# Loading q, k and v in rows of 1 KB, with part of the opening loads moved to ScalarE

## The chip, the cores and the metric

The kernel runs on one core of a Trainium2 chip. The metric is the device time of one execution in microseconds; the median of three runs before the change is 470.75 us (470.01 to 472.14). Engines are called by their short names: PE (TensorE matmuls), PEld (its weight loads), ACT (ScalarE), DVE (VectorE), POOL (GpSimd) and SP (SyncE, which here only issues DMAs; SPq is its sequencer). The engines run their own instruction lists in order and wait for one another through semaphores.

## What is computed

Two layers stand one behind the other. The first is a retention layer without softmax: for 8 batches and 8 heads of 64, over 576 positions, the causal scores are weighted by a power of a per-head decay.

```
scores = scale * q @ k.T
ret    = scores * (gamma ** (i - j) where i >= j else 0)
attn   = ret @ v
```

The second takes that result as `x` (8 x 576 x 512) into a mixture of 4 attention experts, of which each position uses the best 2.

```
w = softmax of the 2 largest of x @ w_gate
for e in range(4):
    q, k, v = x @ wq[e], x @ wk[e], x @ wv[e]
    a = causal softmax(scale * q @ k.T)
    out += w[e] * (a @ v @ wo[e])
```

## The kernel before, in words

The 576 positions of a batch are 9 chunks of 64, and two chunks make a tile. There are 36 tiles (`NT`) of 128 positions, and three tiles make a group, of which there are 12 (`NG`). For each tile n the kernel loads two blocks of 512 KB: `x` (q and k transposed, `load(n, 0)`, tensor `xf`) and `vk` (v and k, `load(n, 1)`, tensor `vkf`). In both, each of 128 partitions receives one run of 4 KB. The pool holds 3 `x` buffers and 4 `vk` buffers, so tile n+3 can only be loaded into `x` when tile n has been read.

The first layer is worked chunk by chunk. `qk(n)` (L130) multiplies q and k of a chunk on PE; ACT copies the result out (`p<-qk`, L144) and POOL zeroes what lies above the diagonal (L147). `decay(n)` (L101) multiplies v by decay factors, on DVE for the first tiles and on POOL later. `state(n)` (L109, `st`) adds a chunk's k-v product to a running sum, kept by DVE (L128). `old(n)` (L152) multiplies q by the sum of all earlier chunks, and ACT copies that out (`x<-old`, L169). `own(n)` (L171) multiplies the chunk's own scores by v, and DVE adds it (L188). `scale(n)` (L200) multiplies by a table `gi`. `split(n)` (L202) rounds the result to a shorter float on ACT (`xh`, L210) and keeps the rest on POOL (`xl`, L211), so that the second layer's projections run as three matmuls each on `xh` and `xl`.

The second layer is a pipeline by group. At stage j, group j-1 is projected (`proj`, `pj`, L250; `vproj`, `pv`, L274), group j-2 goes through scores, softmax and values, and group j-3 through the output projection (`po`, L473), whose tiles SP stores (L477). The opening, called the head here, is j = 0: three tiles of the first layer with no second-layer work on PE. The first `pj` block follows tiles 0 to 2 and needs their `xh` and `xl`, and the weights `k` and `q`, split into `wh` and `wl` by `weights` (ACT L235, then DVE or POOL L236).

Eight PSUM banks go round, mostly two to a step. The first two `pj` outputs take over the two banks of `qk(4)`, so they need ACT's copy `p<-qk` of tile 4.

PE, DVE, ACT and POOL run in the order in which the code writes the work. SP's order is the scheduler's. All loads, of tiles, weights (`fetch`), tables (`gi`, `con`, `mask`) and the gate's weights (`rg`) are issued by SP. Up to eight DMAs are tracked at a time, each by one of eight semaphores: a ninth waits for the first to have landed.

Of the kernel before, what the change touches and what calls it, by code (L numbers as in the profile page):

```python
# [22 lines left out]
NT = 9 * NP  # L23
# [4 lines left out]
def f(ap):  # L28
    return ap.bitcast(F32)
# [9 lines left out]
def units(g):  # L39
    out = []  # L40
    for n in range(3 * g, 3 * g + 3):
        out += [(n, 0), (n, 1)] if n % 9 == 8 else [(n, None)]
    return out
# [3 lines left out]
def kernel(ctx: ExitStack, tc: tile.TileContext, xf, vkf, wraw, gi_d, con_d, out):  # L47
    nc = tc.nc
# [8 lines left out]
    v = nc.vector  # L57
# [25 lines left out]
    HALF = [slice(0, 64), slice(64, 128)]  # L83
    X, VK, P, S_, XR = {}, {}, {}, {}, {}

    def load(n, w):
        if n >= NT:
            return
        if w == 0:
            X[n] = x = ld.tile([128, 2, 4, 128], F32, name="x", tag="x")  # L90
            nc.sync.dma_start(x, xf[n])
        else:
            VK[n] = vk = ld.tile([128, 2, 2, 4, D], F32, name="vk", tag="vk", bufs=4)
            nc.sync.dma_start(vk, vkf[n])

    def table(c):
        t0, C = 128 * c, 128 if c < 4 else 64
# [3 lines left out]
    def decay(n, e=None):  # L101
        if n >= NT:
            return
        vv = VK[n][:, :, 0]
        k = chunks(n)[0][1]
        gm = gam[:, 8:9] if k == 8 else gam[:, k:k + 2]
        (e or gp).tensor_mul(vv, vv, gm.unsqueeze(3).to_broadcast([128, 2, 4, D]))  # L107
# [22 lines left out]
    def qk(n):  # L130
        if n >= NT:
            return
        x = X[n]
        ps = [bank([128, 2, 2, 64], "qk") for g in range(2)]
        for s in range(2):
            i = slice(64 * s, 64 * s + 64)
            for u in range(2):
                for g in range(2):
                    for r in range(2):
                        h = 2 * r + u  # L140
                        mm(ps[g][HALF[r], s, u], x[HALF[g], 1, h, i], x[HALF[g], 0, h, i], start=True, stop=True)  # L141
        P[n] = p = sa.tile([128, 2, 2, 2, 64], F32, name="p", tag="p")
        for g in range(2):
            act(p[:, g], ps[g], AF.Copy)  # L144
        for r in range(2):
            w = p[HALF[r]].rearrange("p g s u i -> p (g s u) i")
            gp.affine_select(w, w, pattern=[[0, 8], [1, 64]], base=0, channel_multiplier=-1,  # L147
                             compare_op=OP.is_ge, fill=0.0)
# [3 lines left out]
    def old(n):  # L152
        if n >= NT:
            return
        ps = [bank([128, 2, 128], "old") for g in range(2)]
        x = X[n]
        R[n] = x32 = sa.tile([128, 2, 2, 128], F32, name="x32", tag="x32", bufs=2)
        ch = chunks(n)
        f0 = 64 if ch[0][1] == 0 else 0
        for s, (b, k) in enumerate(ch):  # L160
            i = slice(64 * s, 64 * s + 64)
            if k:
                for r in range(2):
                    for g in range(2):
                        for u in range(2):
                            mm(ps[g][HALF[u], r, i], S_[b, k - 1][HALF[g], r, u], x[HALF[g], 0, 2 * r + u, i],  # L166
                               start=True, stop=True)
        for g in range(2):
            act(x32[:, g, :, f0:], ps[g][:, :, f0:], AF.Copy)  # L169
# [32 lines left out]
    def split(n, e=None):  # L202
        if n >= NT:
            return
        g, l0 = n // 3, 128 * (n % 3)
        if n % 3 == 0:
            XR[g] = (sa.tile([128, 4, GW], F32R, name="xh", tag="xh"), sa.tile([128, 4, GW], F32R, name="xl", tag="xl"))
        xh, xl = XR[g]
        x32 = R.pop(n).rearrange("p g r i -> p (g r) i")
        act(xh[:, :, l0:l0 + 128], x32, AF.Copy)  # L210
        (e or gp).tensor_sub(xl[:, :, l0:l0 + 128], x32, f(xh[:, :, l0:l0 + 128]))  # L211
# [6 lines left out]
    TSZ = {1: 11 * 128, 2: 15 * 128, 3: 9 * 128, 4: 9 * 128}  # L218
    rg = const.tile([128, 4, E], F32, name="rg")

    def fetch(w):
        o, kc, n = WCUT[w]
        z = {"k": 1, "q": 2, "v": 3, "o": 4}[w]
        RAW[w] = raw = sb.tile([128, PSZ[z]], F32, name="raw", tag=f"p32{z}")[:, :kc * n].rearrange("p (k w) -> p k w", k=kc)
        nc.sync.dma_start(raw, wraw[:, o:o + kc * n].rearrange("p (k w) -> p k w", k=kc))

    def weights(w, e=None):
        o, kc, n = WCUT[w]
        raw = RAW[w]
        wt = n if w != "v" else NWV  # L230
        hi = const.tile([128, kc, wt], F32R, name="wh" + w)
        lo = const.tile([128, kc, wt], F32R, name="wl" + w)
        W[w] = (hi, lo)
        for r, cs in [(raw, slice(0, n))] + ([(rg, slice(n, wt))] if w == "v" else []):
            act(hi[:, :, cs], r, AF.Copy)  # L235
            (e or v).tensor_sub(lo[:, :, cs], r, f(hi[:, :, cs]))  # L236
# [243 lines left out]
    def run(*gs):  # L480
        for g in gs:
            for _ in g:
                pass

    def stage(j, i):
        g, o = j - 1, j - 3
        if 0 <= g < NG:
            if i == (0 if j == 1 else 2):
                for p in range(2):
                    for w in "kq":  # L490
                        yield from proj(g, w, p)
            else:
                for ti in (2,) if i == 1 else (0, 1):
                    yield from vproj(3 * g + ti)
        if 0 <= o < NG and i < 2:
            for d in (2 * i, 2 * i + 1):
                yield from outproj(o, d)
# [8 lines left out]
    load(2, 0)  # L506
    load(2, 1)
    fetch("k")
    fetch("q")
    nc.sync.dma_start(rg, wraw[:, 4096:].rearrange("p (k w) -> p k w", k=4))  # L510
    load(3, 1)
    fetch("v")
    nc.sync.dma_start(mask[:, 512:], con_d[:, 220:])
    decay(0, v)
    qk(0)
    state(0)
    for j in range(NG + 3):
        us = units(j - 2) if 0 <= j - 2 < NG else []
        for i in range(3):
            n = 3 * j + i  # L520
            if n < 2:
                decay(n + 1, v)
            if n != 2:
                qk(n + 1)
            old(n)
            work = stage(j, i)
            here = us[i:i + 1] if i < 2 else us[2:]
            soft = [scores(u) for u in here[:1]]
            for sc in soft:
                next(sc)  # L530
            own(n)
            if n == 2:
                qk(3)
            state(n + 1)
            for u in here[1:]:
                soft.append(scores(u))
                next(soft[-1])
            load(n + 3, 0)
            load(n + 4, 1)
            if n == 0:  # L540
                fetch("o")
            scale(n, v if n < 3 else None)
            if 2 < n + 2 and i < 2:
                decay(n + 2)
            for u, sc in zip(here, soft):
                for _ in sc:
                    next(work, None)
                normal(u)
            split(n)
            if 0 < n + 1 < 5:  # L550
                table(n + 1)
            if i == 2:
                decay(n + 2)
            if n == 1:
                weights("k")
            if n == 2:
                weights("q", gp)
                weights("v")
            if n == 5:
                weights("o")  # L560
            run(work)
        for u in us:
            run(turn(u))
        if 0 <= j - 1 < NG:
            gate(j - 1)
        for u in us:
            values(u, u[0] == NT - 1)


def _layout(inputs):  # L570
    q, k, v = (np.asarray(inputs[n]) for n in "qkv")
    qk = np.stack([q, k], 1).reshape(B, 2, 2, 4, S, D)
    qkt = qk.transpose(0, 2, 5, 1, 3, 4).reshape(B, 128, 2, 4, 9, 64)
    vk = np.stack([v, k], 1).reshape(B, 2, 2, 2, 2, 9, 64, D).transpose(0, 5, 3, 6, 1, 2, 4, 7).reshape(B, 9, 128, 2, 4, D)
    xf = np.stack([np.stack([qkt[b, :, :, :, c] for b, c in chunks(n)], 3) for n in range(NT)]).reshape(NT, 128, 2, 4, 128)
    vkf = np.stack([np.stack([vk[b, c] for b, c in chunks(n)], 1) for n in range(NT)])
    wq, wk, wv = (np.asarray(inputs["moe_w" + n]).transpose(1, 0, 2).reshape(DM, E * D) for n in "qkv")
    wg = np.asarray(inputs["moe_w_gate"])
    wo = np.asarray(inputs["moe_wo"]).reshape(2, 128, DM).transpose(1, 0, 2).reshape(128, 2 * DM)
    cut = [w.reshape(4, 128, -1).transpose(1, 0, 2).reshape(128, -1) for w in (wq, wk, wv, wg)]  # L580
    wraw = np.ascontiguousarray(np.concatenate(cut[:3] + [wo, cut[3]], 1))
    return {"xf": np.ascontiguousarray(xf), "vkf": np.ascontiguousarray(vkf), "wraw": wraw}


def _tables():
# [38 lines left out]
```

## Time and profile before

| what | value |
|---|---|
| median of 3 runs | 470.75 us |
| profiled execution, its own time | 470.5 us |
| its span (first to last instruction) | 468.5 us |
| busy share of the span: PE, PEld, ACT, DVE, POOL | 93%, 85%, 61%, 58%, 46% |
| HBM read | 40.26 MB |
| DMA, mean over the span | 109 GB/s |
| granted clock, mean over the span | 0.967 |

So 2.0 us of the profiled execution lie outside its span. A busy share is a mean over stages with different limits. What the head is worth is read from its own windows, from the chain of waits (which follows the last work back to what released it) and from the timeline, whose rows give the start, the duration, the engine, the line, the operation and, in brackets, the idle time before it with what ended that. "issue" in a chain or a bracket is time in which the engine waited for nothing that the profile shows. Starts are microseconds from the span's beginning.

### The profile page before, as it was taken

What the parts mean: (1) busy time and instruction counts of PE and PEld (TensorE: products, weight loads), DVE (VectorE), ACT (ScalarE), POOL (GpSimd) and SP (SyncE); (2) the same over time, 40 slices, a digit from 0 to 9 for tenths busy, and PEclk for the clock granted to TensorE, in tenths of its full rate; (3) what the DMA queues carried; (4) which work ended last, traced back from release to release, by engine and by line L of the source; (5) the groups of instructions that cost most, each with busy time, mean ns of one, the idle gap of its engine ahead of it and who ended that gap; (6) DMA issues with size and microseconds to landing.
All of it is one profiled execution on the core that took longest, in us unless ns stands there. A gap on an engine that the chain in (4) does not pass through costs nothing.

```text
span 468.5 us, 18762 instructions
## 1 busy us (share of the span) xinstructions
PE 436.8 (93%) x7876; PEld 397.9 (85%) x7876; DVE 273.0 (58%) x1069; ACT 286.4 (61%) x834; POOL 216.1 (46%) x272
## 2 busy tenths in 40 slices
PE   7589879999999999999999999999999999999786
PEld 4478769889879989889979999889979999897476
DVE  1562773864685654864775654854775654746650
ACT  2545466584685476584686576685686576664752
POOL 5477665563653555563653455553553453202001
PEclk8769899999999999999999999999999999999869
DMA  8953441242252153252352153242241010010101
GB/s 286 406 200 105 171 135 48 93 160 91 92 186 65 50 186 110 92 165 86 94 167 83 41 193 111 92 163 88 93 162 44 5 52 18 2 69 2 69 0 69
DMA packets 18899, 50.89 MB, mean 109 GB/s; under 512 B 2304, under 2 KB 9088, under 8 KB 18816
## 3 DMA queue, kind: packets, MB, share of 16 engines
q1 hardware_dynamic: 18816, 49.71, 31.3%
q8 instruction: 62, 1.02, 0.9%
q14 instruction: 21, 0.17, 0.1%
HBM read 40.26 MB, written 9.44 MB: 106 GB/s over the span
## 4 chain that ended last, share of the span: by engine, by line
PE 79%; ACT 7%; DVE 4%; DMA 4%; issue 3%; POOL 1%; SPq 1%; ACTq 0%; POOLq 0%; DVEq 0%
PE pj L250 22%; PE pv L274 11%; PE pt L419 8%; PE po L473 8%; PE ss L348 7%; PE ys L445 6%; PE own L183 4%; DMA x<-xf 4%; PE qk L141 4%; PE st L119 3%; PE old L166 2%; ACT p L379 2%; PE ys L452 2%; DVE sm L391 2%; PE ys L449 2%
## 5 line engine op out<-in xcount | busy, mean ns | idle before, releaser
L211 POOL TENSOR_TENSOR xl<-x,xh 128x512 fp32r<-128x512 f32 x36 | 46.1, 1280 | 89.3 <-ACT xh L210 89.3
L379 ACT ACTIVATE p<-p,nm 128x128 f32<-128x128 f32 (+8 forms) x144 | 79.7, 559 | 10.4 <-DVE nm L368 9.5
L368 DVE CUSTOM_DVE_ANT_0 p<-ss,mask 128x128 f32<-128x128 f32 (+7 forms) x128 | 51.0, 454 | 29.0 <-PE ss L348 28.5
L463 POOL CAST yh<-y 128x256 fp32r<-128x256 f32 (+1 forms) x38 | 14.4, 380 | 106.4 <-ACT y L462 106.4
L399 ACT ACTIVATE p<-p,sm 128x64 f32<-128x64 f32 (+4 forms) x72 | 37.0, 556 | 42.0 <-DVE sm L393 42.0
L423 DVE COPY pth<-pt 128x512 f32<-128x512 f32 (+2 forms) x52 | 31.4, 618 | 48.2 <-PE pt L419 47.8
L147 POOL TENSOR_SCALAR_AFFINE_SELECT p<-p 64x512 f32<-64x512 f32 x72 | 48.7, 676 | 20.3 <-ACT p L144 17.7
L419 PE MATMUL pt<-con,p 128*128 128x128 f32 x360 | 45.1, 287 | 5.4 <-DVE nm L373 3.3
L419 PEld LDWEIGHTS pt<-con,p 128*128 128x128 f32 x360 | 43.3, 149 | 6.1 <-DVE nm L373 3.4
L200 POOL TENSOR_TENSOR x<-x,gi 128x512 f32<-128x512 f32 x29 | 37.4, 1290 | 20.4 <-DVE x L188 19.5
L348 PE MATMUL ss<-k,q 64*64 64x64 f32 (+7 forms) x512 | 41.7, 409 | 2.2 <-ACT ot L476 2.2
L183 PEld LDWEIGHTS own<-p,vk 64*64 64x64 f32 x1152 | 28.5, 142 | 13.4 <-issue 10.4
L445 PE MATMUL ys<-pth,vn 128*64 128x128 f32 (+1 forms) x640 | 39.8, 257 | 0.0
L183 PE MATMUL own<-p,vk 64*64 64x64 f32 x1152 | 30.4, 229 | 6.6 <-ACT xh L210 2.8
L107 POOL TENSOR_TENSOR vk<-vk,con 128x512 f32<-128x512 f32 x33 | 35.4, 1074 | 0.3 <-DMA vk<-vkf 0.3
L391 DVE TENSOR_SCALAR sm<-sm 128x4 f32<-128x4 f32 (+1 forms) x40 | 15.5, 388 | 30.6 <-ACT p L379 30.0
L425 ACT ACTIVATE pth<-pt 128x512 f32<-128x512 f32 (+2 forms) x52 | 27.2, 541 | 9.3 <-PE pt L419 9.3
L210 ACT ACTIVATE xh<-x 128x512 fp32r<-128x512 f32 x36 | 22.2, 617 | 17.2 <-POOL x L200 9.6
L445 PEld LDWEIGHTS ys<-pth,vn 128*64 128x64 f32 x640 | 29.6, 139 | 1.5 <-issue 1.5
L401 DVE TENSOR_SCALAR p<-p,sm 128x64 f32<-128x64 f32 (+4 forms) x104 | 29.1, 333 | 1.4
L141 PEld LDWEIGHTS qk<-x 64*64 64x64 f32 x1152 | 21.6, 141 | 9.6 <-issue 7.0
L119 PE MATMUL st<-vk 64*64 64x64 f32 x1024 | 25.8, 232 | 4.3 <-DVE vk L107 2.2
(94 smaller groups left out, 1069.8 us busy)
## 6 DMA issues: line engine op xcount, KB each, us to landing
x<-xf SPq DMA_DIRECT2D x36, 512.0 KB, 4.0
vk<-vkf SPq DMA_DIRECT2D x36, 512.0 KB, 5.3
out<-ot SPq DMA_DIRECT2D x48, 192.0 KB, 2.0
raw<-wraw SPq DMA_DIRECT2D x4, 512.0 KB, 9.4
gi<-gi SPq DMA_DIRECT2D x1, 256.0 KB, 8.1
con<-con SPq DMA_DIRECT2D x1, 110.0 KB, 3.9
mask<-con SPq DMA_DIRECT2D x1, 32.0 KB, 8.5
rg<-wraw SPq DMA_DIRECT2D x1, 8.0 KB, 9.3
```

What stands on the lines that cost most here:

```text
L119: mm(ps[r][HALF[g], s, u], vk[HALF[r], s, 1, h], vk[HALF[r], s, 0, h], start=True, stop=True)
L141: mm(ps[g][HALF[r], s, u], x[HALF[g], 1, h, i], x[HALF[g], 0, h, i], start=True, stop=True)
L147: gp.affine_select(w, w, pattern=[[0, 8], [1, 64]], base=0, channel_multiplier=-1, compare_op=OP.is_ge, fill=0.0)
L183: mm(ps[r][HALF[u], g, i], vk[HALF[r], s, 0, 2 * g + u], p[HALF[r], g, s, u], start=True, stop=True)
L211: (e or gp).tensor_sub(xl[:, :, l0:l0 + 128], x32, f(xh[:, :, l0:l0 + 128]))
L250: mm(ps, ww[:, kc, p * 128:(p + 1) * 128], xx[:, kc, c], start=(i == 0), stop=(i == 11))
L274: mm(ps, xx[:, kc, l0:l0 + 128], ww[:, kc], start=(i == 0), stop=(i == 11))
L348: mm(ps[e][HALF[p]], q[p][HALF[z], l0 + 64 * s:l0 + 64 * s + 64], k[p][HALF[z], kb:kb + ws[e]], start=True, stop=True)
L368: v.tensor_tensor_reduce(p32[:, e, :ws[e]], ps[e], mask[:, 576 - ws[e]:], -1.0, BIG, OP.add, OP.min, nm[:, e:e + 1])
L379: act(p32[:, e, :ws[e]], p32[:, e, :ws[e]], AF.Exp, bias=bias[e], scale=-1.0, accum_out=sm[:, 0, e:e + 1])
L419: nc.tensor.transpose(pt[:, i], src, ident)
L445: mm(py[HALF[z], p], VN[n0 + j][:, e * D:(e + 1) * D], src, start=(j == 0), stop=False)
```

## The change

Three things are done.

1. The host lays `xf` and `vkf` out so that a tile's block is four pieces of 128 rows of 1 KB, and the loads read them so. A partition still receives 4 KB, as four runs of 1 KB. All 72 loads are changed, over the whole run.
2. At the opening SP issues fewer loads: the blocks of tiles 0 to 3 and the weights `k` and `q`. `x` of tile 3 is now issued in the opening, ahead of the loop.
3. The blocks of tile 4, `rg` and the weight `v` are issued by ACT behind `split(1)`; the blocks of tile 5, `vk` of tile 6 and the weight `o` by ACT behind `split(2)`. From tile 3 on, SP issues the loads at the same places as before. The weight `v` is split into `wh` and `wl` one tile later.

```diff
-    def load(n, w):
+    def load(n, w, e=None):
+        e = e or nc.sync
...
-            nc.sync.dma_start(x, xf[n])
+            e.dma_start(x.rearrange("p a h i -> p (a h i)").rearrange("p (c w) -> p c w", c=4), xf[n].rearrange("c p w -> p c w"))
...
-            nc.sync.dma_start(vk, vkf[n])
+            e.dma_start(vk.rearrange("p s a h d -> p (s a h d)").rearrange("p (c w) -> p c w", c=4), vkf[n].rearrange("c p w -> p c w"))
...
     fetch("k")
     fetch("q")
-    nc.sync.dma_start(rg, wraw[:, 4096:].rearrange("p (k w) -> p k w", k=4))
+    load(3, 0)
     load(3, 1)
-    fetch("v")
     nc.sync.dma_start(mask[:, 512:], con_d[:, 220:])
...
-            load(n + 3, 0)
-            load(n + 4, 1)
-            if n == 0:
-                fetch("o")
+            if n > 2:
+                load(n + 3, 0)
+                load(n + 4, 1)
...
             split(n)
+            if n == 1:
+                load(4, 0, nc.scalar)
+                load(4, 1, nc.scalar)
+                nc.scalar.dma_start(rg, wraw[:, 4096:].rearrange("p (k w) -> p k w", k=4))
+                fetch("v", nc.scalar)
+            if n == 2:
+                load(5, 0, nc.scalar)
+                load(5, 1, nc.scalar)
+                load(6, 1, nc.scalar)
+                fetch("o", nc.scalar)
...
             if n == 2:
                 weights("q", gp)
+            if n == 3:
                 weights("v")
...
+    xf, vkf = (np.ascontiguousarray(a.reshape(NT, 128, 4, 256).transpose(0, 2, 1, 3)) for a in (xf, vkf))
```

The orders below are of one engine each, at three places. Line numbers of the change are one higher than before for the same step.

SP in the opening, before, from `x` of tile 2 to `x` of tile 3 (`raw` is a weight, in the order k and q, v, o):

```order
L91 DMA x<-xf 128x1024
L94 DMA vk<-vkf 128x1024
L225 DMA raw<-wraw 128x1024 x2
L510 DMA rg<-wraw 128x16
L94 DMA vk<-vkf 128x1024
L225 DMA raw<-wraw 128x1024
L513 DMA mask<-con 128x64
L225 DMA raw<-wraw 128x1024
L91 DMA x<-xf 128x1024
```

The same stretch with the change; of the last row's two, the first is `x` of tile 3 and the second `x` of tile 6:

```order
L92 DMA x<-xf 128x4x256
L95 DMA vk<-vkf 128x4x256
L226 DMA raw<-wraw 128x1024 x2
L95 DMA vk<-vkf 128x4x256
L513 DMA mask<-con 128x64
L92 DMA x<-xf 128x4x256 x2
```

Two weights and `rg` no longer stand ahead of `x` of tile 3. All that stands ahead of `x` of tile 2 is as it was.

ACT from `xh` of tile 1 to the copies of tile 2, before:

```order
L210 ACTIVATE xh<-x_312 128x4x128
L99 ACTIVATE gi<-gi,con 128x128 x4
L235 ACTIVATE whk<-raw 128x1024
L169 ACTIVATE x_393<-old 128x256 x2
L144 ACTIVATE p<-qk 128x256 x2
```

and with the change:

```order
L211 ACTIVATE xh<-x_305 128x4x128
L92 DMA x<-xf 128x4x256
L95 DMA vk<-vkf 128x4x256
L552 DMA rg<-wraw 128x16
L226 DMA raw<-wraw 128x1024
L100 ACTIVATE gi<-gi,con 128x128 x4
L236 ACTIVATE whk<-raw 128x1024
```

Four DMA issues now stand on ACT between `xh` of tile 1 and the table, and so ahead of the split of the weight `k`.

ACT from `xh` of tile 2 to the copy of `qk(4)`, before:

```order
L210 ACTIVATE xh<-x_393 128x4x128
L99 ACTIVATE gi<-gi,con 128x128 x4
L235 ACTIVATE whq<-raw 128x1024
L235 ACTIVATE whv<-raw 128x4x256
L235 ACTIVATE whv<-rg 128x4x4
L144 ACTIVATE p<-qk 128x256 x2
```

and with the change:

```order
L211 ACTIVATE xh<-x_389 128x4x128
L92 DMA x<-xf 128x4x256
L95 DMA vk<-vkf 128x4x256 x2
L226 DMA raw<-wraw 128x1024
L100 ACTIVATE gi<-gi,con 128x128 x4
L236 ACTIVATE whq<-raw 128x1024
L145 ACTIVATE p<-qk 128x256 x2
```

Four DMA issues have come in ahead of the copy of `qk(4)`, and the two copies of `whv` have left. On PE and POOL the order is the same as before; on DVE the two steps of `wlv` stand behind the additions of tile 3 instead of ahead of them.

More of the change, by code (lines that the diff above doesn't have):

```diff
@@ L219, with fetch @@
     rg = const.tile([128, 4, E], F32, name="rg")
-    def fetch(w):
+    def fetch(w, e=None):
         o, kc, n = WCUT[w]
@@ L224, in fetch @@
         RAW[w] = raw = sb.tile([128, PSZ[z]], F32, name="raw", tag=f"p32{z}")[:, :kc * n].rearrange("p (k w) -> p k w", k=kc)
-        nc.sync.dma_start(raw, wraw[:, o:o + kc * n].rearrange("p (k w) -> p k w", k=kc))
+        (e or nc.sync).dma_start(raw, wraw[:, o:o + kc * n].rearrange("p (k w) -> p k w", k=kc))
     def weights(w, e=None):
@@ L581, in _layout @@
     wraw = np.ascontiguousarray(np.concatenate(cut[:3] + [wo, cut[3]], 1))
-    return {"xf": np.ascontiguousarray(xf), "vkf": np.ascontiguousarray(vkf), "wraw": wraw}
+    xf, vkf = (np.ascontiguousarray(a.reshape(NT, 128, 4, 256).transpose(0, 2, 1, 3)) for a in (xf, vkf))
+    return {"xf": xf, "vkf": vkf, "wraw": wraw}
 def _tables():
```

## The prediction

> **What bounds the kernel now.** I read first the busy time by stretches, since a share over the whole span hides the head.
>
> ```profile
> core 0: us, PE busy (x) PEld busy (x) DVE busy (x) ACT busy (x) POOL busy (x), PEclk, DMA share, GB/s
> ...
> 12.00:32.00 20.00, 12.51 (x410) 11.46 (x399) 10.33 (x26) 11.68 (x31) 10.98 (x11) 0.66 0.82 315
> 32.00:72.00 40.00, 34.16 (x761) 31.09 (x760) 24.40 (x94) 20.60 (x71) 27.19 (x27) 0.95 0.42 138
> 72.00:390.00 318.00, 312.96 (x5846) 289.42 (x5846) 197.42 (x793) 207.23 (x611) 160.81 (x194) 1.00 0.32 104
> ```
>
> From 72 us on PE is busy for 312.96 of 318 us while DMA is at 0.32. There PE is the bound, a load that takes longer has cover, and whatever the head gains or loses is carried to the end. Only the head has room: from 12 to 32 us PE works 12.51 of 20 us at a granted clock of 0.66, with DMA at 0.82. So I read the chain of waits there.
>
> ```profile
> 3.83 8.66 DMA x<-xf
> 13.32 1.76 issue
> 16.87 8.78 DMA x<-xf
> 25.79 1.12 PE qk L141 x28
> 26.90 1.51 issue
> 31.46 9.00 PE pj L250 x48
> ```
>
> Two loads carry it: x of tile 2, issued at 3.83 and landed at 12.49, and x of tile 4, issued at 16.87 and landed at 25.65. PE starts qk of tile 4 0.14 us after. The first projection, pj, starts at 31.4 us. But a chain shows one limit where there may be two, so I follow ACT, and below it DVE, to the same point.
>
> ```profile
> 20.01 0.63 ACT L210 ACTIVATE xh<-x 128x512 fp32r<-128x512 f32 x1 [2.91 <-DVE x L200]
> 20.55 1.26 ACT L99 ACTIVATE gi<-gi,con 128x128 f32<-128x128 f32 x4
> 21.71 1.04 ACT L235 ACTIVATE whk<-raw 128x1024 fp32r<-128x1024 f32 x1
> ...
> 27.11 0.63 ACT L210 ACTIVATE xh<-x 128x512 fp32r<-128x512 f32 x1 [2.07 <-DVE x L200]
> 27.65 1.26 ACT L99 ACTIVATE gi<-gi,con 128x128 f32<-128x128 f32 x4
> 28.82 1.04 ACT L235 ACTIVATE whq<-raw 128x1024 fp32r<-128x1024 f32 x1
> 29.76 1.04 ACT L235 ACTIVATE whv<-raw 128x1024 fp32r<-128x1024 f32 x1
> ...
> 30.81 0.63 ACT L144 ACTIVATE p<-qk 128x256 f32<-128x256 f32 x2
> ```
>
> ```profile
> 22.79 1.22 DVE L236 TENSOR_TENSOR wlk<-raw,whk 128x1024 fp32r<-128x1024 f32 x1 [2.87 <-ACT whk L235]
> 23.93 0.74 DVE L188 TENSOR_TENSOR x<-x,own 128x256 f32<-128x256 f32 x2
> 25.23 0.88 DVE L128 TENSOR_TENSOR s<-st,s 128x128 f32<-128x128 f32 x4 [0.56 <-PE st L119]
> 26.04 0.98 DVE L200 TENSOR_TENSOR x<-x,gi 128x512 f32<-128x512 f32 x1
> ```
>
> This is a second chain with almost no slack. It goes from xh of tile 1 over whk to DVE's wlk, the additions of own (L188) and st (L128) and scale (L200), and back to ACT's xh of tile 2 and p<-qk of tile 4. Each row starts when the one before ends, but for 0.56 us that DVE waits for st. The first pj needs the bank that p<-qk of tile 4 empties, and starts 0.6 us after that copy. The change puts eight DMA issues on exactly this chain.
>
> **The change part by part.** All sums are made against the profiled execution: 468.5 us of span in 470.5 us, 0.25 us under the median of the runs.
>
> *Rows of 1 KB, transfer.* The trace has no such row, so I take the rows on both sides of it, in three short windows: 4 KB alone, 512-byte rows of gi, 1.5 KB rows of the output.
>
> ```profile
> q1 hardware_dynamic: 561, 2.04, 102.7%
> ...
> DMA packets 390, 0.29 MB, mean 366 GB/s; under 512 B 14, under 2 KB 362, under 8 KB 390
> ...
> q1 hardware_dynamic: 390, 0.29, 109.6%
> ...
> q1 hardware_dynamic: 576, 0.79, 34.9%
> ```
>
> The columns of a queue's row are packets, MB and the share of 16 DMA engines' time. The first window is 5 us: 1.027 x 16 x 5 = 82.2 us of DMA time for 2.04 MB, which is 498 rows of 4 KB (the other packets are tiny and I leave them out): 165 ns each, 1.32 us for a load's 8 rows on each engine. The second is 0.8 us: 14.0 us, less 28 rows of 4 KB at 165, leaves 9.4 us for 348 rows of 512 B, 27 ns. The third is 6 us: 33.5 us for 0.79 MB, 514 rows of 1.5 KB, 65 ns. On the line between, 1 KB is 46 ns, four of them 184 ns, 12% over 165. A load's 32 rows on an engine then take 1.47 us where the queue is full, 0.15 us more. Five loads stand up to and with x of tile 2 (x0, vk0, x1, vk1, x2), none is taken away ahead of it: it lands 0.75 us later, and the chain through it starts 0.75 us later. Bounds: nothing, or 1.1 us if 1 KB costs two rows of 512 B, as gi's.
> A page of the Trainium skill, DMA: Bandwidth & Descriptors (section Why small descriptors are slow), gives a fixed cost of about 3 cycles per packet beside one per 32 bytes. By it four rows of 1 KB take 140 cycles against 131, 7%, and the shift would be an estimated 0.45 us; the rows of gi cost more than that, so I keep the rows.
>
> *Two weights and rg off the opening.* x of tile 3 has two weights less in front (2 x 1.32 us) and eight loads of 1 KB rows (8 x 0.15), so it lands 1.4 us earlier. What that frees:
>
> ```profile
> 21.61 1.05 PE L183 MATMUL own<-p,vk 64*64 64x64 f32 x32 [2.77 <-ACT xh L210]
> 23.23 1.13 PE L141 MATMUL qk<-x 64*64 64x64 f32 x32 [0.56 <-DMA x<-xf]
> 24.11 1.10 PE L119 MATMUL st<-vk 64*64 64x64 f32 x32
> ```
>
> The 0.56 us before qk of tile 3 goes. With the 0.75 above, own starts at 22.36, qk at 23.42, st at 24.30 and ends at 25.4.
>
> *Tile 4 from ACT.* The load is issued with xh of tile 1, at 20.01 + 0.75 = 20.8, when the queue is nearly empty, and lands a lone load's time later.
>
> ```profile
> x<-xf SPq DMA_DIRECT2D x36, 512.0 KB, 4.0
> ```
>
> That is about 25.0, before st of tile 3 ends. qk of tile 4 starts at 25.4, 0.4 us before its 25.79. PE alone would then reach pj 0.4 us earlier, at 31.0. This is all that the change can win here by its loads.
>
> *Eight issues on ACT.* Their price is only seen on SP.
>
> ```profile
> 2.67 0.43 SPq L94 DMA_DIRECT2D vk<-vkf  x1
> 3.14 0.65 SPq L505 DMA_DIRECT2D gi<-gi  x1
> 3.83 1.45 SPq L91 DMA_DIRECT2D x<-xf  x1
> ...
> 16.87 0.33 SPq L91 DMA_DIRECT2D x<-xf  x1
> ```
>
> 128 rows take 0.33 us alone and 0.43 in a series; gi, with 512 rows as each load will have, takes 0.65, and the issue behind it 1.45. A step between two issues costs 0.04. I take gi's own 0.65 for a load and 0.33 for a weight or rg: the first four (x4, vk4, rg, v) 2 x 0.69 + 2 x 0.37 = 2.1 us, the second four (x5, vk5, vk6, o) 3 x 0.69 + 0.37 = 2.45 us. To the second four I add one stall of 1.0 us, as x2 had (1.45 less 0.43): x2 stood behind 72 rows on each of 16 DMA engines (five transfers of 8, and gi's 32), vk6 stands behind 64 and adds 32, more than that; the first four reach 80 only with the last. So 3.45 us. Cheapest: 0.37 an issue, 1.5 us for each four. Dearest: 512 rows cost what gi and its follower took (3.14 to 5.28) less 0.43, 1.7 us; 4.3 and 5.5 us.
>
> The chain again, from its rows: xh of tile 1 at 20.76, the table 2.1 us after at 22.86. Then start to start as before: whk 24.02, wlk 25.10, the addition of own 26.24 for 0.74, the addition of st (no wait now) 26.98, scale 27.79, xh of tile 2 at 28.86. Then 3.45 us of issues to 32.3, the table 1.17 to whq at 33.5, whq 0.94 to p<-qk at 34.4 (both copies of whv are gone), and 0.6 to pj: **35.0 us, against 31.4: 3.6 us later.** What this chain has to give (0.56 of waiting for st, whv's 1.05) is already used in it.
>
> *From tile 3 on.* whv and wlv one tile later, then 1.0 us of ACT and up to 2.7 of DVE, beside the 9.00 us of pj: nothing. Loads at the old places: a landing of 4.0 us grows by some tenths, and a buffer's turn is a tile, 468.5 us for 36 tiles, 13 us: nothing. If that cover is gone, PE waits 0.2 us per load. Sum: 470.5 + 3.6 = **474.1 us**.
>
> **The rivals.** *A, PE's own path decides.* The issues are cheap, or ACT's sequencer does them inside the 2.91 and 2.07 us in which it waits for scale. Then the ACT chain is at 35.0 less 2.55 (5.55 us of issues less twice 1.5), 32.45, or earlier, and PE's at 31.0: 470.1 to 471.6. For it: issues of 0.33 are the common ones. Against: xh waits for DVE and the issues stand behind it in order; the row of gi.
> *B, faster: instruction fetch.* PE's stalls of 1.76, 2.77 (put down to xh) and 1.51 us each come as a packet of instructions is fetched, in the midst of full DMA queues.
>
> ```profile
> q8 instruction: 62, 1.02, 0.9%
> ...
> q8 instruction: 1, 0.02, 3.8%
> ```
>
> ```profile
> 55.36 0.92 PE L119 MATMUL st<-vk 64*64 64x64 f32 x32 [0.96 <-issue]
> ```
>
> The second row is of 12.0 to 13.7 us: 3.8% of 16 x 1.7 is 1.03 us for 16 KB. If shorter rows and a thinner queue let such packets through sooner, each stall could fall to the 0.96 us of the one at 55 us, where DMA is at 0.42: 6.04 less 2.88, 3.2 us in all, and 466.9 with the 0.4 above. Against: the packet itself takes its 1.03 us, PE resumes well after it, and ACT's chain must be free as well.
> A rule of the Trainium skill, Runtime: NRT & Kernel Launch (Instruction fetch mechanics), holds that fetch is hidden, since dispatch is slower than the refill. By it B is worth nothing; the trace disagrees in the head, with 1.76 us of issue where the packet runs.
> *C, slower still: a load of 512 rows holds the issuer for 1.7 us.* The place is the same, the price 4.3 + 5.5 in place of 5.55 us: 4.2 us more, 478.3. It decides as soon as the second load of a series is delayed like x2. For it: x2's 1.45. Against: gi's own 0.65.
> The Trainium skill, Perfetto Trace Analysis (DMA Optimizations), warns of transfers under 2 KB; that speaks against the change, and for C's side.
>
> **How the numbers follow.** My forecast 0.50, of it 472 to 477; A 0.27; B 0.08; C 0.15. The range of 8 in 10 reaches from 470.0 (A, without the row's price) to 478.5 (C). What a measurement can tell from no change is 0.5%, 2.35 us: faster means under 468.4, slower over 473.1. Slower holds C and most of the forecast, 0.15 + 0.40 = 0.55; the same, A and the rest, 0.36; faster 0.09.
>
> **What would show it.** In the profile after: x of tile 2 lands 0.5 to 1 us later; the wait of qk of tile 3 for its load is gone; ACT is idle between xh and the table for 1.5 us behind tile 1 and near 3 behind tile 2; p<-qk of tile 4 starts near 34.4 and pj near 35; the windows from 72 us on are as before. If ACT's gaps are under 0.5 us, A holds; if PE's stalls as issue shrink, B. If PE's idle time after 72 us changes, the rows of 1 KB reach further than I think.

## The result and the profile after

The changed kernel takes 477.28 us (median of 4 runs, 472.67 to 478.69) against 470.85 us (470.01 to 472.14) for the kernel before on the same chip: a ratio of 1.0113, 95% interval 1.0074 to 1.0151. Timed once more, unaltered, it took 476.22 us against 472.42, ratio 1.006 (1.002 to 1.010). It is slower, by 0.6 to 1.1%. A ratio leaves out executions over 1.5% above their kernel's fastest (one of the change's second timing, two of the moved issues with rows of 4 KB), so it can be lower than the quotient of the medians, which hold all. The forecast was slower, with 474.1 us and a range of 470.0 to 478.5.

The profile kept of the changed kernel is of its shortest execution: 472.67 us, a span of 470.9. Busy time by stretches, as the prediction showed it of the kernel before:

```profile
core 0: us, PE busy (x) PEld busy (x) DVE busy (x) ACT busy (x) POOL busy (x), PEclk, DMA share, GB/s
...
12.00:32.00 20.00, 10.99 (x385) 9.82 (x384) 9.38 (x25) 8.15 (x23) 9.37 (x11) 0.76 0.72 241
32.00:72.00 40.00, 34.61 (x720) 31.91 (x724) 19.66 (x82) 20.93 (x71) 26.32 (x26) 0.90 0.53 173
72.00:390.00 318.00, 311.89 (x5866) 287.81 (x5862) 197.95 (x795) 207.44 (x611) 160.70 (x194) 1.00 0.33 105
```

The loss is in the head. From 12 to 32 us the trace has 385 matmuls of PE and not 410, though DMA has a lighter load and the granted clock is higher (0.76 against 0.66). From 72 us on PE is busy as before (311.89 of 318 us, before 312.96). From 32 to 72 us the clock is lower, 0.90 where it was 0.95.

The chain of waits (start, duration, what) no longer runs over the load of tile 4. It goes from the load of tile 2 into DVE and ACT:

```profile
4.20 9.27 DMA x<-xf
14.31 1.94 issue
21.37 0.45 ACT xh L211
23.46 0.16 ACT gi L100
24.74 0.95 ACT whk L236
29.09 0.41 ACT xh L211
31.39 0.16 ACT gi L100
32.67 0.94 ACT whq L236
33.94 10.05 PE pj L251 x48
```

x of tile 2 lands at 13.47 (before 12.49). The first pj starts at 33.94 and not at 31.4. What lies between ACT's rows is in ACT's timeline, with its DMA issues (ACTq):

```profile
21.37 0.63 ACT L211 ACTIVATE xh<-x 128x512 fp32r<-128x512 f32 x1 [3.44 <-DVE x L201]
21.40 0.43 ACTq L92 DMA_DIRECT2D x<-xf  x1
21.92 0.46 ACTq L95 DMA_DIRECT2D vk<-vkf  x1
22.42 0.52 ACTq L552 DMA_DIRECT2D rg<-wraw  x1
22.97 0.44 ACTq L226 DMA_DIRECT2D raw<-wraw  x1
23.46 1.27 ACT L100 ACTIVATE gi<-gi,con 128x128 f32<-128x128 f32 x4 [1.46 <-issue]
...
25.59 0.63 ACT L170 ACTIVATE x<-old 128x256 f32<-128x256 f32 x2
...
29.11 0.39 ACTq L92 DMA_DIRECT2D x<-xf  x1
29.59 1.02 ACTq L95 DMA_DIRECT2D vk<-vkf  x2
30.66 0.69 ACTq L226 DMA_DIRECT2D raw<-wraw  x1
31.39 1.28 ACT L100 ACTIVATE gi<-gi,con 128x128 f32<-128x128 f32 x4 [1.68 <-issue]
...
33.52 0.63 ACT L145 ACTIVATE p<-qk 128x256 f32<-128x256 f32 x2
```

From the start of xh to that of the table gi it took 0.54 us before (20.01 to 20.55, 27.11 to 27.65). Now it takes 2.09 us behind tile 1 and 2.30 us behind tile 2, which the four issues fill back to back; the first of them still runs beside xh. ACT's arithmetic is idle for 1.46 and 1.68 us of it, put down to "issue". PE meanwhile waits three times for others:

```profile
26.00 1.38 PE L142 MATMUL qk<-x 64*64 64x64 f32 x32 [2.46 <-ACT x L170]
32.18 1.23 PE L120 MATMUL st<-vk 64*64 64x64 f32 x32 [2.55 <-POOL vk L108]
33.94 1.65 PE L251 MATMUL pj<-xh,whk 128*128 128x384 f32 x4 [0.53 <-ACT p L145]
```

qk of tile 4 does not wait for its load, which ACT issued at 21.40 and which landed at 25.46. It waits for a bank: with eight banks and two to a step it takes over those of tile 2's old products, and ACT's first copy out of them ends at 25.95. That copy (`x<-old`) stands behind the split `whk`, and so behind the four issues. Before, it came 3 us earlier, long before the load:

```profile
22.66 0.63 ACT L169 ACTIVATE x<-old 128x256 f32<-128x256 f32 x2
```

st of tile 4 waits for POOL's decay of vk, which stands in POOL's order behind xl of tile 2, and so behind ACT's late xh. And pj waits for ACT's p<-qk.

### The profile page after: what moved, and what is told of

The parts are those of the page before. It is cut to its first block, busy times and chain, and to the rows that moved or that the text cites. A ratio compares the mean times of both kernels' runs of the same rounds, so it can differ in the third digit from the quotient of the medians.

```text
span 470.9 us, 18762 instructions
## 1 busy us (share of the span) xinstructions
PE 436.1 (93%) x7876; PEld 395.5 (84%) x7876; DVE 270.3 (57%) x1069; ACT 286.6 (61%) x834; POOL 215.1 (46%) x272
## 4 chain that ended last, share of the span: by engine, by line
PE 76%; ACT 8%; DVE 6%; issue 3%; DMA 2%; POOL 2%; ACTq 1%; SPq 1%; DVEq 0%; POOLq 0%
PE pj L251 22%; PE pv L275 10%; PE pt L420 8%; PE po L474 8%; PE ss L349 6%; PE ys L446 6%; PE own L184 4%; PE qk L142 3%; PE st L120 3%; PE old L167 2%; ACT p L380 2%; DMA x<-xf 2%; PE ys L453 2%; PE ys L450 2%; DVE sm L392 1%
## 5 line engine op out<-in xcount | busy, mean ns | idle before, releaser
L380 ACT ACTIVATE p<-p,nm 128x128 f32<-128x128 f32 (+8 forms) x144 | 79.7, 559 | 10.4 <-DVE nm L369 9.5
L424 DVE COPY pth<-pt 128x512 f32<-128x512 f32 (+2 forms) x52 | 31.3, 618 | 47.9 <-PE pt L420 47.4
L148 POOL TENSOR_SCALAR_AFFINE_SELECT p<-p 64x512 f32<-64x512 f32 x72 | 47.6, 661 | 21.9 <-ACT p L145 19.3
L420 PE MATMUL pt<-con,p 128*128 128x128 f32 x360 | 43.2, 279 | 6.5 <-DVE nm L374 3.3
L420 PEld LDWEIGHTS pt<-con,p 128*128 128x128 f32 x360 | 41.4, 144 | 7.5 <-DVE nm L374 3.4
L349 PE MATMUL ss<-k,q 64*64 64x512 f32 (+7 forms) x512 | 42.3, 410 | 2.2 <-ACT ot L477 2.2
L392 DVE TENSOR_SCALAR sm<-sm 128x4 f32<-128x4 f32 (+1 forms) x40 | 14.1, 354 | 30.9 <-ACT p L380 30.4
L189 DVE TENSOR_TENSOR x<-x,own 128x256 f32<-128x256 f32 (+1 forms) x72 | 25.4, 385 | 9.6 <-ACT x L170 5.8
L402 DVE TENSOR_SCALAR p<-p,sm 128x64 f32<-128x64 f32 (+4 forms) x104 | 29.1, 332 | 1.4
```

Source lines behind the costliest of these rows:

```text
L349: mm(ps[e][HALF[p]], q[p][HALF[z], l0 + 64 * s:l0 + 64 * s + 64], k[p][HALF[z], kb:kb + ws[e]], start=True, stop=True)
L380: act(p32[:, e, :ws[e]], p32[:, e, :ws[e]], AF.Exp, bias=bias[e], scale=-1.0, accum_out=sm[:, 0, e:e + 1])
L420: nc.tensor.transpose(pt[:, i], src, ident)
```

## The experiments

Every kernel was timed beside the kernel before on the same chip. The table gives the start of the first pj and the time from there to qk of tile 5, which stands behind its 48 matmuls, both from the one profiled execution.

| kernel | median us | ratio to before (95%) | first pj | pj to qk of tile 5 |
|---|---|---|---|---|
| before | 470.85, 472.42, 471.82, 471.46 | | 31.4 | 9.0 |
| the change | 477.28 | 1.0113 (1.0074 to 1.0151) | 33.9 | 10.0 |
| the change once more | 476.22 | 1.006 (1.002 to 1.010) | 34.6 | 10.1 |
| rows of 1 KB alone | 473.77 | 1.0024 (1.0004 to 1.0044) | 32.7 | 8.7 |
| the moved issues, rows of 4 KB | 474.08 | 1.0013 (0.9986 to 1.004) | 33.5 | 11.0 |
| second four issues later | 475.46 | 1.0063 (1.0034 to 1.0091) | 32.9 | 10.6 |
| the change, issues by SP | 473.21 | 1.0032 (1.0009 to 1.0055) | 33.3 | 8.6 |
| issues by SP, rows of 4 KB | 470.70 | 0.9968 (0.9935 to 1.0000) | 31.3 | 10.4 |
| four more issues on ACT | 477.92 | 1.0127 (1.0084 to 1.0170) | 37.2 | 10.9 |
| five and seven filling matmuls | 477.02 | 1.0101 (1.0062 to 1.0141) | 33.7 | 10.7 |
| sixteen filling matmuls | 475.39 | 1.0069 (1.0038 to 1.0100) | 34.4 | 8.6 |
| decay ahead of xl | 470.68 | 0.9982 (0.9954 to 1.0010) | 29.7 | 8.6 |
| the same, and unit 33 turned early | 470.09 | 0.9975 (0.9949 to 1.0001) | 30.5 | 9.0 |

### The change once more, and its two halves

The changed kernel was run unaltered:

> The changed kernel unaltered, for its spread: its four executions so far took 472.7 to 478.7 us, and the one with a trace was the shortest. If the cost is only ScalarE's issues and the rows (a later first projection, some 2.5 us in that trace), the runs centre on 473. If a second effect takes part in most executions, they centre on 477, and the longer ones show a lower granted clock (0.95 to 0.96 against 0.974).

It took 472.64 to 479.84 us: a spread of 7 us, where the kernel before beside it went from 469.99 to 475.33. The forecast had no term for that spread. The expectation's "second effect" with a lower clock is there. It is taken up below.

Rows of 1 KB alone, all loads issued by SP in the places of before:

```
-            nc.sync.dma_start(x, xf[n])
+            nc.sync.dma_start(x.rearrange(...).rearrange("p (c w) -> p c w", c=4), xf[n].rearrange("c p w -> p c w"))
```

> The kernel before with rows of 1 KB alone, all issues on SyncE in their old order. By the forecast's terms: x of tile 2 lands 0.75 us later, x of tile 4 (ten loads of 1 KB rows ahead and with it, at 0.15) 1.5 us later, so the first projection starts 1.5 us later, 472.0 us; nothing changes after 72 us. If the rows reach the whole run (the second effect), 476 us or more. If rows cost nothing, 470.8.

473.77 us, ratio 1.0024. In its chain of waits the two loads are still there, the first longer than before (9.32 against 8.66 us), the second as long (8.69 against 8.78):

```profile
4.13 9.32 DMA x<-xf
18.49 8.69 DMA x<-xf
32.72 8.68 PE pj L250 x48
```

x of tile 2 lands at 13.45, 0.96 us later than before, and pj starts 1.3 us later. The rows cost about that and no more; the reading that they slow the whole run (476 or more) falls.

The other half, the moved issues with rows of 4 KB:

```
-            e.dma_start(x.rearrange(...), xf[n].rearrange("c p w -> p c w"))
+            e.dma_start(x, xf[n])
```

> The change with rows of 4 KB: loads thinned and eight issues on ScalarE, nothing else. By the forecast: x of tile 2 lands at 12.5 as before, four issues behind tile 1 take 1.6 to 2.1 us and four behind tile 2 as much; the first projection starts 1.5 to 2 us later than before, 472 to 472.5 us. If ScalarE's issues are the second effect, 476 us or more here and not with the rows alone.

474.08 us, a ratio of 1.0013 that holds no change as well. The first pj is at 33.5, 2.1 us later than before, a little more than expected. Its chain of waits has one issue on ACT of 1.37 us (L552, rg), and behind it 11.08 us of pj:

```profile
21.30 1.37 ACTq L552
33.47 11.08 PE pj L251 x48
```

This kernel also shows best that the bank holds up qk of tile 4: its load landed at 24.53, ACT's first copy ended at 25.70, and qk started at 25.75.

Neither half alone gives the whole. By the medians of that series (before 472.42) they cost 1.35 and 1.66 us, together 3.0; the change cost 3.8.

### Where ACT's issues stand

The second four issues moved behind the copies of tile 3's old products, so that p<-qk of tile 4 goes ahead of them:

```
             old(n)
+            if n == 3:
+                load(5, 0, nc.scalar)
+                load(5, 1, nc.scalar)
+                load(6, 1, nc.scalar)
+                fetch("o", nc.scalar)
...
-            if n == 2:
-                load(5, 0, nc.scalar)
-                load(5, 1, nc.scalar)
-                load(6, 1, nc.scalar)
-                fetch("o", nc.scalar)
```

> The change with the second four issues on ScalarE moved from behind tile 2 to behind the copies of tile 4's qk and tile 3's old, that is off the chain to the first projection. By the forecast that chain gets shorter by their 2.3 us in the trace (29.11 to 31.39), until PE itself is the limit: the first projection at 32.0 to 32.7 against 33.94, 471 us. If the issues behind tile 2 do not decide, no change from the changed kernel.

pj starts at 32.9, 1.0 to 1.7 us earlier than in the two profiles of the change, just outside the 32.0 to 32.7 that were expected. The chain of waits shows what holds it there:

```profile
28.66 0.64 ACT xh L211
30.66 1.05 POOL vk L108
31.75 1.23 PE st L120 x31
32.98 10.57 PE pj L251 x48
```

Not ACT now but POOL: xl waits for xh, the decay of vk waits behind xl, st waits for that, and pj stands right behind st. The time fell by 0.8 us only and not to 471, and this kernel's mean clock was the lowest of this series (0.9605; the kernel before had 0.9677). By the fit below, at equal clock, it stands 1.7 us over the kernel before, where the change stands 3.3 over it.

The counter-test, all eight late issues at the same places of the program, but on SP:

```
-                load(4, 0, nc.scalar)
+                load(4, 0)
...
-                fetch("o", nc.scalar)
+                fetch("o")
```

> The change with one part undone: the eight late transfers stand at the same places of the program, but SP issues them and not ACT; rows of 1 KB and the short opening stay. Forecast's theory (the issues on ACT hold up xh, whk, whq and p<-qk of tile 4): the first pj starts at 31.6 to 32.3 us in place of 33.9 to 34.6, and the time falls from the 476.2 of the changed kernel to 472.8 to 473.8, about that of the rows alone (473.8). If it is not ACT but the order of the loads that costs, pj stays above 33 and the time at 475 to 477.

473.21 us: as expected by the forecast's theory, the time of the rows alone. pj is later than expected: 33.3, which was to speak for the order of the loads as the cost. ACT goes from xh to the table at once again. What is late is PE: qk of tile 4 starts right behind its load, which lands at 27.44 (25.65 before, 27.19 with the rows alone), and has 1.78 us of stall in its midst (1.51 before):

```profile
28.46 0.63 ACT L211 ACTIVATE xh<-x 128x512 fp32r<-128x512 f32 x1 [2.08 <-DVE x L201]
28.99 1.26 ACT L100 ACTIVATE gi<-gi,con 128x128 f32<-128x128 f32 x4
```

```profile
27.58 1.12 PE L142 MATMUL qk<-x 64*64 64x64 f32 x28 [1.02 <-DMA x<-xf]
30.48 0.37 PE L142 MATMUL qk<-x 64*64 64x64 f32 x2 [1.78 <-issue]
...
33.31 0.97 PE L251 MATMUL pj<-xh,whk 128*128 128x384 f32 x4
```

So the time drops without the issues on ACT, and the late pj is due to the loads; with full clock its 48 matmuls also take 8.6 us and not 10.0. It is not a test of the short opening: SP's order is the scheduler's, and it put tile 3's x behind the weights again, as before. The same with rows of 4 KB (both edits together) is then nearly the kernel before, but for the copy of whv one tile later:

> The short opening alone: rows of 4 KB as before, all transfers issued by SP, two weights, rg and x of tile 4 behind tile 1, the last weight and x5, vk5, vk6 behind tile 2. Forecast's theory: without the price of the rows and of the issues only PE's own path is left, pj at 31.0 to 31.6 (before: 31.4) and 471.5 to 472.6, within 0.2% of the kernel before. If the short opening is what costs, pj above 32.5 and 473.5 or more.

470.70 us, ratio 0.9968, pj at 31.30 as expected. These four kernels form a square: rows of 4 or 1 KB, issues by SP or ACT. They are put together below.

The other direction, four more issues on ACT behind tile 2, of 8 KB each, into a buffer that nothing reads:

```
                 fetch("o", nc.scalar)
+                for t in range(4):
+                    nc.scalar.dma_start(spare[:, t], wraw[:, 4096:].rearrange("p (k w) -> p k w", k=4))
```

> The change, and behind tile 2 four more issues on ACT that move 8 KB each into a buffer that nothing reads. ACT's issues took 0.39 to 0.69 us each with 0.04 between. If ACT's chain sets pj with slope one: pj 2.0 to 2.4 us later than in the changed kernel (36.0 to 37.0), the time up by 2.0 to 2.4, 478.2 to 478.6. If PE's or POOL's path decides pj: under 0.5 us, 476.2 to 476.7.

477.92 us, 1.7 us over the second timing of the change, where 2.0 to 2.4 were expected; the mean of 6 runs is uncertain by 0.8. ACT's timeline shows the 2.12 us, and a single issue of 1.67 behind tile 1 that is not part of the edit:

```profile
23.07 1.67 ACTq L227 DMA_DIRECT2D raw<-wraw  x1
...
32.54 2.12 ACTq L561 DMA_DIRECT2D spare<-wraw  x4
34.70 1.28 ACT L100 ACTIVATE gi<-gi,con 128x128 f32<-128x128 f32 x4 [3.66 <-DMA x<-xf]
```

pj started at 37.2, 2.6 to 3.3 us after the change's and just past the expected 37.0: the 2.1 and that long issue. Issue time on ACT in the head went to pj nearly one to one in this execution. In the time it is less sure: at equal clock, by the fit below, this kernel stands 4.0 us over the kernel before (standard error 0.5) and the change 3.3.

### The clock

The spread had a pattern. The executions with a low mean granted clock were the long ones (correlation -0.96 over the 8 runs of the second timing, -0.77 over the 31 of the kernel before beside them). In the trace the granted clock is either full or half, and switches on a grid of 3.41 us whose start differs from execution to execution. Cut at that grid, the kept execution of the change reads:

```profile
core 0: us, PE busy (x) PEld busy (x) DVE busy (x) ACT busy (x) POOL busy (x), PEclk, DMA share, GB/s
...
23.24:26.66 3.42, 0.96 (x47) 0.75 (x38) 0.94 (x1) 3.20 (x9) 0.11 (x1) 1.00 0.99 324
26.66:30.07 3.41, 2.97 (x83) 2.49 (x72) 2.33 (x8) 0.73 (x2) 1.51 (x3) 0.50 0.33 118
30.07:33.48 3.41, 1.23 (x32) 1.04 (x32) 0.00 (x0) 2.09 (x5) 2.06 (x2) 0.50 0.95 305
33.48:36.90 3.42, 2.96 (x9) 2.96 (x10) 1.54 (x6) 1.22 (x5) 3.14 (x3) 0.50 1.05 359
36.90:40.31 3.41, 3.41 (x21) 3.41 (x21) 0.00 (x0) 1.51 (x6) 3.33 (x4) 1.00 0.73 256
```

PE is busy for 0.96 us of the first window, and the next has half the clock; 1.23 us of the third, and the fourth, in which pj has begun, has half the clock. Nine pj matmuls run in that window and 21 in the next. Over all 13 traces, of 76 windows in which PE was busy for less than half, 72 were followed by one at half clock; of 1,514 in which it was busy for 80% or more, 7 were. The Trainium skill, TensorE: Matmul & The Clock Gate (section What's actually happening), describes such a gate with a free-running window of 3413 ns; these traces agree. Its rule, no idle gap of PE over some 3.4 us (section HAM oscillation), is too mild here: gaps of 1.8 to 2.6 us were enough.

If that is a cause, filling the gap ahead of st of tile 4 must keep pj at full clock. First with five and seven matmuls of a zero tile into the bank that own, then st, overwrites at once:

```
         ps = [bank([128, 2, 2, D], "st") for r in range(2)]
+        for t in range(7 if n == 4 else 0):
+            mm(ps[0].rearrange("p s u d -> p (s u d)"), wz, wz[:, None, :].to_broadcast([128, 2, 128]), ...)
```

> The change, and matmuls of a zero tile that fill PE's idle time: five into own's bank ahead of own of tile 2, seven into st's bank ahead of st of tile 4, in the 1.7 and 1.8 to 2.6 us in which PE waits there for p and vk; what they write is overwritten. Second theory (found after the forecast): a clock window of 3.4 us in which PE is busy for less than half is followed by one at half clock, and so the wait ahead of st puts the first pj at half clock. Then pj starts as in the changed kernel (33.9 to 34.6), its 48 matmuls take 9.0 to 9.4 us in place of 10.05 to 10.2, and the time falls by 0.8 to 1.7 us, 474.5 to 475.4. If the half clock does not come from PE's idle time: pj at 10 us or more, 476.2 to 476.7.

This did not do it: 477.02 us, and pj at half clock as before. The filling ran at full clock and was over after 0.94 us, with 1.86 us of idle time behind it, so the window stayed below half busy:

```profile
28.47 0.94 PE L116 MATMUL st<-wz 128*128 128x256 bf16 x7
31.27 1.07 PE L122 MATMUL st<-vk 64*64 64x64 f32 x32 [1.86 <-POOL vk L108]
```

Then with sixteen, ahead of st alone:

> The change, with sixteen matmuls of a zero tile ahead of st of tile 4 and none elsewhere (five and seven had run at full clock and were over after 0.9 us, so the window stayed below half busy). At full clock they take about 2.1 us, at half clock 3.9; what they write is overwritten, and pj waits for p<-qk of tile 4 anyway. Clock theory: the window ahead of pj is then busy for more than half, pj's 48 matmuls take 9.0 to 9.6 us and not 10.0 to 10.4, and the time at like clock elsewhere is 0.5 to 1.3 us lower: 475 to 476 against the 476.2 to 477.0 of the change. If idle time of PE does not set the clock: pj at 10 us or more and 477 or above.

Here the window that the filling falls into is full (3.41 of 3.41 us), the clock comes back at 31.77, and pj has it from its first matmul:

```profile
28.36:31.77 3.41, 3.41 (x65) 2.74 (x58) 0.14 (x1) 0.63 (x1) 2.27 (x2) 0.50 0.57 155
31.77:35.19 3.42, 2.34 (x44) 1.94 (x43) 0.00 (x0) 3.30 (x9) 1.05 (x1) 1.00 1.01 334
```

pj to qk of tile 5 took 8.6 us against 10.0 to 10.1, with pj at 34.4 as in the change. The time, 475.39 us, is where it was expected, but 0.8 us under the change's 476.22 is less than the two intervals can tell apart. So the trace shows the mechanism in one execution each; the gain in time is not shown.

To set the two causes apart I laid one straight line through all 199 timed runs of both kernels and the variants (the series not told apart): a constant for each kernel, plus one slope for the time at half clock (the span times twice the missing clock). The slope is 0.20 us per us at half clock (standard error 0.014), and at equal clock the kernels stand to the kernel before so, each with a standard error of about 0.35 us:

| | rows of 4 KB | rows of 1 KB |
|---|---|---|
| issues by SP | -1.0 | +1.0 |
| issues by ACT | +1.3 | +3.3 |

Rows cost 2.0 us in both lines (1.3 where they are the only edit), ACT's issues 2.3 us in both columns. Since SP's loads also stand in another order than ACT's, the 2.3 is the price of both together. Besides, the changed kernel spends 33.1 us at half clock, the kernel before 29.1: 4.0 times 0.20 is 0.8 us more. 3.3 and 0.8 make the 4.1 us between the means of all their runs (476.11 and 472.00). A fit shows that the times go with the clock; that idle PE sets it rests on the windows above.

### Towards a faster kernel

The second four issues showed that POOL's order ties st to ACT. With SP's issues and rows of 4 KB I put the decay of tile 4's vk ahead of xl of tile 2:

```
+            if n == 2:
+                decay(4)
             split(n)
...
-            if i == 2:
+            if i == 2 and n > 2:
                 decay(n + 2)
```

> A candidate: 4 KB rows, all transfers issued by SP, the copy of whv behind tile 3 as in the change, and on POOL the decay of vk of tile 4 ahead of xl of tile 2. In the run of 4 KB rows with SP's issues, st of tile 4 waited 1.18 us for that decay and pj came right behind st (31.30), while p<-qk of tile 4 was done by 30.3. If POOL's order was the last limit: st near 29.0, pj at 30.3 to 30.6, 0.7 to 1.0 us less, ratio to the kernel before 0.993 to 0.997. If vk of tile 4 lands too late or xl is then missed by pj: no change, ratio 0.997 to 1.000.

st follows own without a wait and pj starts at 29.7, 1.7 us earlier than before and more than expected:

```profile
28.55 0.73 PE L120 MATMUL st<-vk 64*64 64x64 f32 x30
29.66 0.97 PE L251 MATMUL pj<-xh,whk 128*128 128x384 f32 x4 [0.38 <-ACT p L145]
```

The median is 470.68, ratio 0.9982, which cannot be told from no change, and by the fit (-0.7) it is no better than the same kernel without this edit (-1.0). In the kept execution, the shortest of twelve, the lead is still there at the last pj block (411.8 against 413.7 before); over all executions it does not show, and why stays open. Adding, at the end of the program, the transposes of unit 33 ahead of the scores of tile 35:

```
+            if i == 2 and j == NG + 1:
+                run(turn(us[0]))
             soft = [scores(u) for u in here[:1]]
...
-        for u in us:
+        for u in us[1 if j == NG + 1 else 0:]:
             run(turn(u))
```

> The same candidate, and at the end of the program the transposes of unit 33 ahead of the scores of tile 35, where PE else waits 3.3 us for nm behind those scores. Clock theory: the window at 438 to 442 us is then busy for over half, the transposes and values after it run at full clock more often, and three copies of pth leave the end: 1.5 to 3 us less than the candidate without it, ratio to the kernel before 0.988 to 0.993, mean clock up by 0.004 to 0.010. If DVE's and ACT's work alone sets the end: under 0.7 us and the clock as it was.

470.09 us, ratio 0.9975 (0.9949 to 1.0001), and 0.6 us under the candidate without it, with the clock as it was: by the expectation, DVE's and ACT's work sets the end. The gap has only moved, since the scores now wait for the banks that DVE has still to empty:

```profile
443.03 1.20 PE L357 MATMUL ss<-k,q 64*64 64x512 f32 x14 [2.39 <-DVE pth L424]
```

By their ratios to the kernel before, both versions are 0.8 to 1.4% faster than the changed kernel; neither beats the kernel before by more than a measurement can tell.

## Why the prediction was right, and where it was off

**Slower, by ACT's chain: right.** The step that decided the sign, eight issues on the chain from xh to p<-qk, is what the runs show: with the same issues on SP the time is 1.0032 of before and not 1.006 to 1.011, and four more issues put pj later still.

**Rows of 1 KB: right in kind, too small.** Predicted 0.75 us on x of tile 2, measured 0.98 (0.96 with the rows alone). In the full queue two loads landed 1.45 to 1.55 us apart instead of 1.27 to 1.34, some 0.2 us more a load where the sum had 0.15. SP also reaches x of tile 2 later, at 4.20 and not at 3.83; whether that adds anything while the queue is full is not shown. The 0.45 us estimated from the Trainium skill's page DMA: Bandwidth & Descriptors (section Why small descriptors are slow) was further off. In time the rows cost 1.3 to 2.0 us at equal clock.

**Two weights less: right.** The 0.56 us ahead of qk of tile 3 is gone; its load landed at 21.01 and not at 23.09.

**Tile 4 from ACT: the load right, PE's own path wrong.** The load landed at 25.46 (predicted 25.0) and qk of tile 4 started at 26.0 (25.4). The step by which PE alone reaches pj at 31.0 failed, since PE is tied to ACT in two places that it left out. qk of tile 4 needs the bank of tile 2's old products, which ACT empties behind whk, and st of tile 4 needs POOL's decay, which stands behind xl and so behind ACT's xh. With the second four issues moved out of the way, pj still came at 32.9. I had followed ACT and DVE to pj, not POOL, and of the banks only the one of p<-qk.

**The price of the issues: the first four right, the second four too dear in this execution.** Predicted 2.1 and 3.45 us from xh to the table. Measured 2.09 behind tile 1 and 2.30 behind tile 2: the long issue of 1.0 us that I had added did not come there. In other executions it came: in the second profile of the change the table starts 3.27 us behind xh (28.79 and 32.06), and with the sixteen filling matmuls two issues took 2.04 us. The same loads are issued in all of them, with SP's falling among ACT's a little differently, so the count of rows from which I had argued for that issue does not settle when it comes. So the chain reached xh of tile 2 at 29.09 (predicted 28.86), p<-qk at 33.5 (34.4) and pj at 33.94 (35.0), and at 34.60 in the second profile: 2.5 to 3.2 us later than before, not 3.6. And the second four did not add in full: in the kept execution st, behind POOL, ended at 33.4, so pj at 33.94 is only 0.5 us later than PE and POOL allowed.

**From tile 3 on nothing: right, with one term missing.** From 72 us on PE is as busy as before. But pj itself took 1.0 us longer, because the later wait of PE put it into a window of half clock; the sum of 474.1 had no clock in it. By the timeline, the second block of pj starts 3.3 us later than before (75.0 and 71.7) and the last 3.9 us later (417.6 and 413.7); the kept execution then won 1.4 us back in the last stretch, where its clock was 0.98 against 0.93. That the direct part agrees, 3.6 predicted and 3.3 measured at equal clock, is partly luck: pj came earlier than predicted and took longer. By the start of qk of tile 5, behind pj, the two profiles are 3.5 and 4.4 us late. The clock's 0.8 us on top is what the forecast lacked. Part of the rest of the distance from 474.1 to the 476.2 of the second timing is that the kernel before took 472.4 beside it, and not the 470.5 from which the sum was made.

**The rivals.** A, PE's path decides, falls: ACT's gaps are 1.46 and 1.68 us, and without the issues the time drops. B, faster fetch, falls, since nothing got faster: the stall ahead of old of tile 2 is 1.94 and 1.45 us in the two profiles, against 1.76, and in qk of tile 4 the second has 1.34 against 1.51. C, 1.7 us for an issue of 512 rows, falls for ACT, where the longest such issue in any trace took 1.39; on SP, in the full opening, single ones took up to 2.72.

## What to carry to other kernels

A DMA issue cost its engine 0.4 to 0.5 us in which it starts nothing else: four of them ahead of a copy that others wait for were 1.5 to 2.8 us of delay, whatever the data was for. Follow every engine in front of the block that matters, the lightly loaded one too, and every bank that must first be emptied; here POOL's in-order list and a bank of ACT's tied PE to ACT. And when a gap of PE moves, look at what runs in the 3 us after it, since that may run at half clock.

## What the runs showed of the hardware

- The granted clock of this one core is full or half in windows of 3.41 us whose grid starts elsewhere in each execution. Under half a window of PE work was followed by half clock in 72 of 76 cases. The time of one program goes with it (correlation -0.77 with the mean clock over 31 runs of the kernel before, whose times span 5 to 6 us in each of the three larger series).
- An issue of 512 rows of 1 KB took 0.37 to 0.38 us alone on SP, 0.43 to 0.51 in a series and up to 2.72 in the full queue of the opening; on ACT 0.39 to 0.69, and in some executions one of 1.08 to 1.39. The row count alone did not set it: on ACT rg, with 8 KB in 128 rows, took 0.52, and a weight, in 128 rows of 4 KB, 0.44 to 1.67.
- With rows of 1 KB two loads landed 1.45 to 1.55 us apart in the full queue, and 1.27 to 1.34 with rows of 4 KB.
- x of tile 4, the first load of its series on ACT, landed 4.07 us after its issue; the median of the x loads from SP is 4.0. The three vk loads on ACT, later in their series, have a median of 7.9 against 5.5 from SP, so no run here tells the engine apart from the place in the series.
